# First gate and up weights in two transfers of two contraction blocks each, ahead of the index table, in a fused spectral and gated-MLP kernel

## The chip, the cores and the metric

The kernel runs on one core of a Trainium2 chip. The metric is the device time of one execution in microseconds. Before the change the median of 8 runs is 178.51 us (178.4 to 178.95). A profile is one further execution, recorded by the hardware profiler; its times are counted from the start of its span.

## The reference, cut to what matters

```python
xn = _layernorm(x, axis=-1)                       # x: 2048 x 512
# branch A: a filter in the frequency domain
X = jnp.fft.rfft2(xn.astype(jnp.float32), axes=(-2, -1))
A = jnp.fft.irfft2(X * (w_r + 1j * w_i), s=(2048, 512), axes=(-2, -1))
# branch B: a gated MLP, w_gate and w_up 512 x 1792, w_down 1792 x 512
g = jnp.einsum("bsd,df->bsf", xn, w_gate)
u = jnp.einsum("bsd,df->bsf", xn, w_up)
B = jnp.einsum("bsf,fd->bsd", gelu(g) * u, w_down)
return x + A + B
```

## The kernel before

The 2048 rows are cut into 16 "columns" c of 128 rows each (row 16 p + c lies on partition p). A column of x is 128 x 512 in bf16, 128 KB. Four columns make one block `sb` of 512 rows. The hidden width of 1792 is cut into 14 blocks f of 128, the contraction over 512 into 4 blocks e of 128.

**Branch B.** For each row block and each f, TensorE (PE) forms `g_ps` and `u_ps`, each as four matmuls over e (line 490; line 498 for the very first unit, which runs e 0 and 1 for all its blocks and then e 2 and 3). ScalarE (ACT) turns `g_ps` into `ge` (line 503), VectorE (DVE) multiplies `u_ps` by `ge` into `hT` (line 508). After the whole of this and of branch A, the down projection `y_ps` (line 817) runs over the 14 blocks, the last step of branch A is added into the same PSUM tile (line 821), DVE adds x (line 824), and SyncE (SP) stores.

**Branch A.** The two-dimensional transform and its inverse are chains of small matmuls `bp`, `dp`, `ep`, `gp`, `yp`, with copies on ACT, multiplications by the filter tables `TW` on DVE, and an exchange of partition halves by DMA (line 729). The tables are gathered on GpSimd (POOL) with the row numbers in `idx_t` (line 594).

**Who decides the order.** A planner (`Plan`, lines 135 to 198) takes every step with its engine, its estimated duration, its key and a due time `t_min`, and writes out a static order for each engine. `LAND`, `WG_LAND`, `WU_LAND` and `RF_LAND` (lines 308 to 312) are the landing times that it assumes for the x columns, the weights and a table. They are not waits of the program: those are on semaphores. The list `todo` (line 532) gives the units of branch B: first column 0 with f 0 to 3, then column 1 with f 0 to 3, columns 0 and 1 with f 4 to 5 and with f 6 to 7, then columns 2 and 3 with f 0 to 7 in pairs, columns 0 to 3 with f 8 to 13, and after that the other row blocks.

**The opening.** SP issues all loads, on one hardware queue, in the order of lines 281 to 306: columns 0 and 1 (one each), the index table, gate weights of f 0 to 3 for all four e (512 KB), the up weights of the same (512 KB), columns 2 and 3, gate and up weights of f 4 to 7 (512 KB each), further columns, the weights of f 8 to 13 (768 KB each), and then the remaining columns and tables. The program gives these transfers eight completion semaphores in turn, so a transfer is issued after the one eight places ahead of it has landed.

Meanwhile PE runs 37 filler matmuls on zeros (line 320); DVE takes mean and variance of column 0 and of column 1 (lines 339 and 342) and normalizes (line 345); PE transposes (line 351), DVE copies the result into `xnT` (line 354), and six more filler matmuls follow column 0 (line 324). Columns 2 and 3 go the same way a little later, with the reciprocal root on POOL (lines 357 and 361). The later columns are transposed by DMA (line 455).

Of the kernel before, what the change touches and what calls it, by code (L numbers as in the profile page):

```python
# [10 lines left out]
P = 128  # L11
# [3 lines left out]
ALU = mybir.AluOpType  # L15
AF = mybir.ActivationFunctionType
# [3 lines left out]
NC = 16  # L20
NG = 8
NE = 4
DF = 1792
NFC = DF // P
NSB = 4
EPS = 1e-5
# [108 lines left out]
class Plan:  # L135
# [6 lines left out]
    def add(self, eng, occ, fn, deps=(), key=0.0, lat=None, slack=0.0, t_min=0.0, acq=(), rel=(), after=None):  # L142
        lat = occ + 0.25 if lat is None else lat
        op = Op(len(self.ops), eng, occ, lat, fn, [d for d in deps if d is not None], key, slack, t_min, acq, rel,
                after)
        self.ops.append(op)
        return op
# [54 lines left out]
def kernel(  # L202
# [11 lines left out]
    nc = tc.nc  # L214
    const_np, ccols, rf_np, ri_np, idx_np = _tables()
    cap = nc.inline_tensor(const_np, name="spec_consts").ap()
    rf_d = nc.inline_tensor(rf_np, name="spec_rf").ap()
# [14 lines left out]
    Wg_sb = pc.tile([P, NE, DF], BF16, name="Wg_sb")  # L232
    Wu_sb = pc.tile([P, NE, DF], BF16, name="Wu_sb")
# [6 lines left out]
    W = 257  # L240
# [7 lines left out]
    def load_consts(first, last):  # L248
        a, b = ccols[first][0], sum(ccols[last])
        nc.sync.dma_start(out=CT[:, a:b], in_=cap[:, a:b])  # L250


    def load_x(c0, n, eng=nc.sync):
        eng.dma_start(out=x_t[:, c0:c0 + n, :], in_=x_v[:, c0:c0 + n, :])

    def load_w(a, b, eng=nc.sync):
        nc.sync.dma_start(out=Wg_sb[:, :, a:b], in_=wg_v[:, :, a:b])
        eng.dma_start(out=Wu_sb[:, :, a:b], in_=wu_v[:, :, a:b])
# [1 line left out]
    eps_t = pc.tile([P, 1], F32, name="eps_t")  # L260
    spin = pc.tile([P, P], BF16, name="spin")
    warm = pc.tile([P, 1], F32, name="warm")
    nc.vector.memset(spin[:], 0.0)
    nc.vector.memset(eps_t[:], EPS)
    minus_half = pc.tile([P, 4], F32, name="minus_half")
    nc.vector.memset(minus_half[:], -0.5)
    ident_t = pc.tile([P, P], BF16, name="ident_t")
    nc.gpsimd.memset(ident_t[:], 1.0)
    nc.gpsimd.affine_select(out=ident_t[:], in_=ident_t[:], pattern=[[-1, P]], compare_op=ALU.is_equal, fill=0.0,
                            base=0, channel_multiplier=1)  # L270

    def load_x(c0, n, eng=nc.sync):
        return eng.dma_start(out=x_t[:, c0:c0 + n, :], in_=x_v[:, c0:c0 + n, :])  # L273

# [1 line left out]
        v = wg_v if T is Wg_sb else wu_v  # L276
        return eng.dma_start(out=T[:, e, a:b], in_=v[:, e, a:b])  # L277

    pin = tc.keep_in_program_order
    pin(nc.scalar.activation(out=warm[:], in_=eps_t[:], func=AF.Sqrt, bias=eps_t[:], scale=1.0))  # L280
    pin(load_x(0, 1))
    pin(load_x(1, 1))
    idx_t = pc.tile([P, 3], I32, name="idx_t")
    nc.sync.dma_start(out=idx_t[:], in_=nc.inline_tensor(idx_np, name="spec_rows").ap())  # L284
    load_w(Wg_sb, 0, 512)
    load_w(Wu_sb, 0, 512)
    load_x(2, 2)
    load_w(Wg_sb, 512, 1024)
    load_w(Wu_sb, 512, 1024)
    load_x(4, 2)  # L290
    load_x(6, 2)
    load_w(Wg_sb, 1024, DF)
    load_w(Wu_sb, 1024, DF)
    load_x(8, 2)
    load_x(10, 2)
    for c in range(0, NC, 8):
        nc.sync.dma_start(out=RF_t[:, c:c + 8], in_=rf_d.rearrange("p (c k) -> p c k", c=NC)[:, c:c + 8])
    load_x(12, 2)
    load_x(14, 2)
    load_consts("F0", "L0")  # L300
    load_consts("I0", "M0")
    for T, w_in in ((TR, A_w_r), (TI, A_w_i)):
        rows = w_in.rearrange("(kb a h g) k -> h kb a (g k)", kb=NC, h=2, a=8)
        Tf = T.rearrange("p j k -> p (j k)")
        for h in range(2):
            nc.sync.dma_start(out=Tf[64 * h:64 * h + 64, W:8 * W], in_=rows[h, :, 0:4, W:8 * W])

    LAND = {0: 2.9, 1: 3.6, 2: 8.4, 3: 8.4}
    LAND.update({c: 11.5 if c < 8 else 17.5 if c < 12 else 20.5 for c in range(4, NC)})
    WG_LAND = [6.3] * 4 + [10.2] * 4 + [13.2] * 6  # L310
    WU_LAND = [7.4] * 4 + [11.7] * 4 + [15.2] * 6
    RF_LAND = 19.0

    ident = ident_t[:]
# [1 line left out]
    IQ = [cc(f"I{q}") for q in range(4)]  # L316

    sp_ps = ps.tile([P, D], F32, name="sp_ps", tag="S", bufs=4)
    for k in range(37):
        pin(nc.tensor.matmul(sp_ps[:, :P], lhsT=spin[:], rhs=spin[:], start=True, stop=True))  # L320

    def spin_on():
        for k in range(6):
            nc.tensor.matmul(sp_ps[:, :P], lhsT=spin[:], rhs=x_t[:, 0, :P], start=True, stop=True)
# [3 lines left out]
    add = plan.add  # L328
# [8 lines left out]
    def f_stats(c):  # L337
        tiles["st", c] = st = pw.tile([P, V.BN_STATS_DIM], F32, name="stats", bufs=4)
        V.bn_stats(out=st[:], in_=x_t[:, c, :])  # L339
# [34 lines left out]
    def first_two():  # L374
        o = {}

        def v(k, fn, occ, deps=(), lat=None, t_min=0.0):
            o[k] = add("DVE", occ, fn, [o[d] for d in deps], key=-2000 + len(o), lat=lat, t_min=t_min,
                       after=o.get("last"))
            o["last"] = o[k]  # L380

        def T(c, h):
            o["T", c, h] = add("PE", 0.12, lambda: f_T(c, 2 * h, 2), [o["xn", c, h]], key=-2000 + 2 * c + h,
                               lat=0.36, acq=("S",))

        def xn_(c, h):
            v(("xn", c, h), lambda: f_norm_v(c, 256 * h, 256), 0.27, [("recip", c)], lat=0.4)

        def stats(c):
            v(("stats", c), lambda: f_stats(c), 0.6, t_min=LAND[c], lat=0.7)  # L390

        def mean(c):
            v(("mean", c), lambda: f_mean(c), 0.17, [("stats", c)])
            o["root", c] = add("ACT", 0.31, lambda: A.activation(
                out=rstd[:, c:c + 1], in_=mv[:, c, 1:2], func=AF.Sqrt, bias=eps_t[:], scale=1.0),
                [o["mean", c]], key=-2000 + c)

        def recip(c):
            v(("recip", c), lambda: V.reciprocal(out=rstd[:, c:c + 1], in_=rstd[:, c:c + 1]), 0.15, [("root", c)])

        stats(0)
        mean(0)
        stats(1)

        recip(0)
        xn_(0, 0)
        mean(1)
        xn_(0, 1)
        T(0, 0)
        T(0, 1)  # L410
        add("PE", 0.33, spin_on, [o["T", 0, 1]], key=-1500, lat=0.33, after=o["T", 0, 1])
        table = add("ACT", 1.3, lambda: None, [o["root", 1]], key=-1500, lat=1.3)
        v("copy0", lambda: f_Tc(0, 0, 2), 0.25, [("T", 0, 0)], lat=0.4)
        o["copy0"].rel = ("S",)
        xT_op[0, 0] = o["copy0"]
        recip(1)
        v("copy1", lambda: f_Tc(0, 2, 2), 0.25, [("T", 0, 1)], lat=0.4)
        o["copy1"].rel = ("S",)
        xT_op[0] = o["copy1"]
        xn_op[0] = o["xn", 0, 1]  # L420
        v("xn1", lambda: f_norm_v(1, 0, D), 0.33, [("recip", 1)], lat=0.45)
        t = add("PE", 0.23, lambda: f_T(1, 0, NE), [o["xn1"]], key=-1998, lat=0.45, acq=("S",))
        o["t"] = t
        v("copyt", lambda: f_Tc(1, 0, NE), 0.5, ["t"])
        o["copyt"].rel = ("S",)
        xT_op[1] = o["copyt"]
        xn_op[1] = o["xn1"]

    ROOT = 1.1
    first_two()  # L430

    def moments(c, key):
        s = add("DVE", 0.6, lambda: f_stats(c), key=key, t_min=LAND[c] if c < 4 else max(LAND[c], 14.7))
        return add("DVE", 0.1, lambda: f_mean(c), [s], key=key - 0.5)

    def second_two():
        m = [moments(c, -1200 + c) for c in (2, 3)]
        m = add("POOL", ROOT, lambda: root_eps(2, 2), m, key=-1190, lat=ROOT + 0.1)
        for c in (2, 3):
            xn_op[c] = add("DVE", 0.33, lambda c=c: f_norm_v(c, 0, D), [m], key=-1180 + c, lat=0.53)  # L440
            t = add("PE", 0.23, lambda c=c: f_T(c, 0, NE), [xn_op[c]], key=-880 + c, lat=0.5, acq=("S",))
            e, f = ("ACT", A.copy) if c == 2 else ("DVE", V.tensor_copy)
            xT_op[c] = add(e, 0.5, lambda c=c, f=f: f_Tc(c, 0, NE, f), [t], key=-1100 + c, rel=("S",))
# [26 lines left out]
    def unit(k, c0, n, f0, m=1):  # L470
# [41 lines left out]
        def split(name, tag, W_, key, t, h):  # L512
            o = None
            for f in range(0, m, h):
                o = add("PE", occ * h / m, lambda f=f: mm(name, tag, W_, range(f, f + h)), [o] if f else src, key=key,
                        lat=occ * h / m + 0.3, acq=() if f else (tag,), t_min=t[f0 + f + h - 1])
            return o
# [3 lines left out]
            g = add("PE", occ / 2, lambda: mm_half(1), [xT_op[0], g], key=1000.1, lat=occ / 2 + 0.3)  # L521
        else:
            g = split("g_ps", "G", Wg_sb, 1000 + k, WG_LAND, m)
        u = split("u_ps", "U", Wu_sb, 1003.1 if k == 2 else 1000.5 + k, WU_LAND, (2, m, 1)[k] if k < 3 else m)
        ge = add("ACT", {1: 0.28, 2: 0.36, 4: 0.5}[n * m], f_ge, [g], key=-1000 + k,
                 lat={1: 0.38, 2: 0.48, 4: 0.7}[n * m], acq=("ge",), rel=("G",))
        h = add("DVE", {1: 0.21, 2: 0.34, 4: 0.61}[n * m], f_h, [ge, u], key=-1000 + k, rel=("U", "ge"))
# [318 lines left out]

    E_ = mybir.EngineType
    with tc.manual_schedule(engines={E_.PE, E_.DVE, E_.Activation, E_.Pool, E_.SP}):
        for op in plan.order():
            op.fn()  # L850

# [29 lines left out]
```

## Time and profile before

| | |
|---|---|
| median of 8 runs | 178.51 us |
| the profiled execution | 178.73 us |
| its span | 177.0 us |
| granted TensorE clock | 1.00 |
| instructions | 3114 |
| HBM read, written | 13.38 MB, 2.10 MB |

How to read it: "busy" is the time in which an engine had an instruction running. PEld is PE's weight load, which runs beside its matmuls. A name such as `L490 PE MATMUL u_ps<-xnT,Wu_sb` gives line, engine, operation, and output and inputs by the program's names; `x264` counts instructions. Behind an arrow stands what ended an idle time. In the windows view each row is a stretch of the span, with the busy time of PE, PEld, DVE, ACT and POOL and the instructions of each in brackets, then the granted clock, the mean busy share of the 16 DMA engines, and what they moved in GB/s. "SPq" is the queue in which SP issues transfers; "to landing" is the time from an issue to the completion of its transfer. The chain is the work that ended last, followed back from the last instruction.

### The profile page before, as it was taken

The numbers are of one execution on the slowest core, as the hardware profiler recorded it, in microseconds if no ns is written. First come the engines' busy times: TensorE is split into PE (matmuls) and PEld (weight loads), VectorE is DVE, ScalarE is ACT, GpSimd is POOL, SyncE is SP. The second block draws the span as 40 slices with busy tenths as digits, with TensorE's granted clock in tenths as the row PEclk, the third lists the DMA queues.
The fourth block names the chain that finished last, engine by engine and source line by source line (L and its number), as shares of the span: only waits on it lengthen the run. The fifth ranks groups of instructions, "written<-read, shape, count | busy, mean of one in ns | idle before, by whom it ended". The sixth has DMA issues, their size and how long they took to land.

```text
span 177.0 us, 3114 instructions
## 1 busy us (share of the span) xinstructions
PE 171.5 (97%) x1127; PEld 96.7 (55%) x1145; DVE 116.0 (66%) x255; ACT 95.9 (54%) x170; POOL 17.2 (10%) x38
## 2 busy tenths in 40 slices
PE   7899999999999999999999999999999999999993
PEld 7698845455544554555555455454445445444463
DVE  3588999987434599979899999643516325344333
ACT  4442489799746988898899964362112111211200
POOL 1020340505760000000000000000000000000000
PEclk9999999999999999999999999999999999999999
DMA  3999997433817802211201520200122222221212
GB/s 91 354 378 377 377 180 120 89 62 72 254 34 227 310 0 59 59 30 35 59 17 44 138 61 15 59 0 4 58 90 89 76 76 61 78 99 60 79 43 59
DMA packets 21871, 19.35 MB, mean 109 GB/s; under 512 B 8480, under 2 KB 20000, under 8 KB 21856
## 3 DMA queue, kind: packets, MB, share of 16 engines
q1 hardware_dynamic: 21440, 17.84, 35.3%
q0 software_dynamic: 416, 1.32, 2.6%
q8 instruction: 9, 0.15, 0.3%
q14 instruction: 6, 0.05, 0.1%
HBM read 13.38 MB, written 2.10 MB: 87 GB/s over the span
## 4 chain that ended last, share of the span: by engine, by line
PE 93%; DMA 3%; SPq 1%; issue 1%; DVE 0%
PE u_ps L490 27%; PE y_ps L817 27%; PE g_ps L490 27%; DMA Wu_sb<-in_B_w_up_dram 3%; PE yp L768 2%; PE gp L738 2%; PE dp L635 2%; PE bp L577 2%; PE y_ps L821 2%; PE ep L644 2%; SPq L273 0%; PE tp L351 0%; SPq L277 0%; SPq L284 0%; DVE y_sb L824 0%
## 5 line engine op out<-in xcount | busy, mean ns | idle before, releaser
L490 PE MATMUL u_ps<-xnT,Wu_sb 128*128 128x512 bf16 (+2 forms) x264 | 56.5, 340 | 0.5
L490 PE MATMUL g_ps<-xnT,Wg_sb 128*128 128x512 bf16 (+2 forms) x252 | 55.8, 349 | 0.2
L817 PE MATMUL y_ps<-Wd_sb,hT 128*128 128x512 bf16 (+2 forms) x246 | 50.6, 355 | 0.3
L508 DVE TENSOR_TENSOR hT<-u_ps,ge 128x512 bf16<-128x512 f32 x56 | 38.4, 688 | 18.2 <-PE u_ps L490 15.7
L503 ACT ACTIVATE ge<-g_ps 128x512 bf16<-128x512 f32 x56 | 33.7, 601 | 24.5 <-PE g_ps L490 21.4
L490 PEld LDWEIGHTS <-Wu_sb 128*128 128x128 bf16 x272 | 24.9, 98 | 21.0 <-DMA Wu_sb<-in_B_w_up_dram 0.3
L817 PEld LDWEIGHTS <-hT 128*128 128x128 bf16 x252 | 23.2, 98 | 22.4
L490 PEld LDWEIGHTS <-Wg_sb 128*128 128x128 bf16 x256 | 24.0, 98 | 20.6
L774 ACT CAST yf<-yp 128x512 bf16<-128x512 f32 x16 | 9.3, 586 | 40.5 <-PE yp L768 40.5
L824 DVE TENSOR_TENSOR y_sb<-y_ps,y_sb 128x512 bf16<-128x512 f32 (+2 forms) x18 | 11.1, 631 | 30.1 <-PE y_ps L821 30.1
L649 ACT CAST E<-ep 64x512 bf16<-64x512 f32 x32 | 18.5, 579 | 1.4 <-PE ep L644 1.0
L339 DVE BATCH_NORM_STATS2 stats<-x_t 128x6 f32<-128x512 bf16 x16 | 10.3, 673 | 2.4 <-DMA x_t<-in_A_x_dram 2.4
L452 ACT ACTIVATE xn<-x_t,nb,rstd 128x512 bf16<-128x512 bf16 x12 | 9.5, 811 | 1.0 <-POOL nb L370 1.0
L547 ACT CAST ds<-dp 128x512 bf16<-128x512 f32 x16 | 9.2, 597 | 0.8 <-PE dp L635 0.8
L547 ACT CAST Gs<-gp 128x512 bf16<-128x512 f32 x16 | 8.7, 591 | 0.6 <-PE gp L738 0.5
L547 ACT CAST Bs<-bp 128x512 bf16<-128x512 f32 x16 | 8.3, 607 | 0.5 <-PE bp L577 0.5
L780 DVE TENSOR_TENSOR lv<-yf 128x512 bf16<-128x512 bf16 x16 | 6.1, 421 | 1.5 <-ACT yf L774 0.7
L768 PEld LDWEIGHTS <-Gs 128*128 128x128 bf16 x64 | 4.8, 98 | 3.5
L787 DVE TENSOR_TENSOR yt<-lv 128x512 bf16<-128x512 bf16 x16 | 6.1, 421 | 0.3
L768 PE MATMUL yp<-CT,Gs 128*128 128x128 bf16 x64 | 6.0, 219 | 0.1
L821 PE MATMUL y_ps<-yt,RI_t 128*128 128x512 bf16 (+2 forms) x18 | 6.1, 355 | 0.0
L559 DVE TENSOR_TENSOR A<-xn 128x1024 bf16<-128x1024 bf16 x8 | 5.2, 675 | 1.0 <-ACT xn L452 1.0
(65 smaller groups left out, 119.1 us busy)
## 6 DMA issues: line engine op xcount, KB each, us to landing
F<-F SPq DMA_DIRECT2D x32, 64.0 KB, 2.0
y_sb<-in_A_x_dram SPq DMA_DIRECT2D x16, 128.0 KB, 2.1
out_dram<-y_sb SPq DMA_DIRECT2D x15, 128.0 KB, 1.7
x_t<-in_A_x_dram SPq DMA_DIRECT2D x7, 256.0 KB, 8.9
Wd_sb<-in_B_w_down_dram SPq DMA_DIRECT2D x1, 1792.0 KB, 7.7
Wg_sb<-in_B_w_gate_dram SPq DMA_DIRECT2D x2, 512.0 KB, 5.4
Wu_sb<-in_B_w_up_dram SPq DMA_DIRECT2D x2, 512.0 KB, 6.4
Wg_sb<-in_B_w_gate_dram SPq DMA_DIRECT2D x1, 768.0 KB, 9.9
```

The lines of the kernel that those rows point to most:

```text
L339: V.bn_stats(out=st[:], in_=x_t[:, c, :])
L452: xn_op[c] = add("ACT", 0.72, lambda c=c: A.activation(out=xn[:, c, :], in_=x_t[:, c, :], func=AF.Identity, bias=nb[:, c:c + 1], scale=rst ...
L490: T_.matmul(b[name][:, f], lhsT=W_[:, e, (f0 + f) * P:(f0 + f + 1) * P], rhs=rhs[:, e, :], start=(e == 0), stop=(e == NE - 1))
L503: A.activation(out=b["ge"][:], in_=b["g_ps"][:], func=AF.Gelu_apprx_tanh)
L508: V.tensor_tensor(out=hT_of(sb, f0, m, o, w), in0=b["u_ps"][:], in1=b["ge"][:], op=ALU.mult)
L547: A.copy(out=o, in_=i)
L649: A.copy(out=b["E"][64 * h:64 * h + 64, r], in_=b["ep", h][64 * r:64 * r + 64])
L768: T_.matmul(t[:, q], lhsT=late["G"][:, q, c0 + j], rhs=IQ[q], start=(q == 0), stop=(q == 3), skip_group_check=True)
L774: A.copy(out=b["yf"][:, j], in_=b[j][:])
L817: T_.matmul(b[o][:], lhsT=hT_of(sb, f, 1, cl * P, P)[:, 0], rhs=Wd_sb[:, f, o:o + w], start=(f == 0), stop=False)
L821: T_.matmul(b[o][:], lhsT=late["RI"][:, c, :], rhs=late["yt"][:, c, o:o + w], start=False, stop=True)
L824: V.tensor_tensor(out=b["y"][:, o:o + w], in0=b[o][:], in1=b["y"][:, o:o + w], op=ALU.add)
```

## The change

The weights of f 0 to 3 are loaded in two transfers of two e blocks (256 KB) for the gate and two for the up matrix. The index table is loaded after the x columns, the table `RF` in one transfer where there were two, and the last four x columns in one where there were two. All fills, loads and filler matmuls of the opening are put into a function that runs at the start of the hand-scheduled region. The planner gets other landing times for the first columns and weights; the key of unit 2's up half becomes that of the other units; and the statistics of columns 2 and 3 are ordered behind the last copy of column 1.

```diff
-    pin(load_x(0, 1))
-    pin(load_x(1, 1))
-    nc.sync.dma_start(out=idx_t[:], in_=nc.inline_tensor(idx_np, name="spec_rows").ap())
-    load_w(Wg_sb, 0, 512)
-    load_w(Wu_sb, 0, 512)
-    load_x(2, 2)
...
-    for c in range(0, NC, 8):
-        nc.sync.dma_start(out=RF_t[:, c:c + 8], in_=rf_d.rearrange("p (c k) -> p c k", c=NC)[:, c:c + 8])
-    load_x(12, 2)
-    load_x(14, 2)
...
-    LAND = {0: 2.9, 1: 3.6, 2: 8.4, 3: 8.4}
+    def opening():
+        nc.vector.memset(spin[:], 0.0)
...
+        nc.scalar.activation(out=warm[:], in_=eps_t[:], func=AF.Sqrt, bias=eps_t[:], scale=1.0)
+        load_x(0, 1)
+        load_x(1, 1)
+        for e in range(0, NE, 2):
+            load_w(Wg_sb, 0, 512, e=slice(e, e + 2))
+        for e in range(0, NE, 2):
+            load_w(Wu_sb, 0, 512, e=slice(e, e + 2))
+        load_x(2, 2)
+        load_w(Wg_sb, 512, 1024)
+        load_w(Wu_sb, 512, 1024)
+        load_x(4, 2)
+        load_x(6, 2)
+        load_w(Wg_sb, 1024, DF)
+        load_w(Wu_sb, 1024, DF)
+        load_x(8, 2)
+        load_x(10, 2)
+        nc.sync.dma_start(out=RF_t[:], in_=rf_d.rearrange("p (c k) -> p c k", c=NC))
+        load_x(12, 4)
+        nc.sync.dma_start(out=idx_t[:], in_=nc.inline_tensor(idx_np, name="spec_rows").ap())
...
+        for k in range(37):
+            nc.tensor.matmul(sp_ps[:, :P], lhsT=spin[:], rhs=spin[:], start=True, stop=True)
+
+    LAND = {0: 2.9, 1: 3.6, 2: 7.2, 3: 7.2}
     LAND.update({c: 11.5 if c < 8 else 17.5 if c < 12 else 20.5 for c in range(4, NC)})
-    WG_LAND = [6.3] * 4 + [10.2] * 4 + [13.2] * 6
-    WU_LAND = [7.4] * 4 + [11.7] * 4 + [15.2] * 6
+    WG_LAND = [5.0] * 4 + [8.6] * 4 + [13.2] * 6
+    WU_LAND = [6.2] * 4 + [10.0] * 4 + [15.2] * 6
...
-        m = [moments(c, -1200 + c) for c in (2, 3)]
+        m = [moments(c, -1200 + c, chain_end) for c in (2, 3)]
...
-        u = split("u_ps", "U", Wu_sb, 1003.1 if k == 2 else 1000.5 + k, WU_LAND, (2, m, 1)[k] if k < 3 else m)
+        u = split("u_ps", "U", Wu_sb, 1000.5 + k, WU_LAND, (2, m, 1)[k] if k < 3 else m)
...
     with tc.manual_schedule(engines={E_.PE, E_.DVE, E_.Activation, E_.Pool, E_.SP}):
+        opening()
         for op in plan.order():
             op.fn()
```

More of the change, by code (lines that the diff above doesn't have):

```diff
@@ L262 @@
     warm = pc.tile([P, 1], F32, name="warm")
-    nc.vector.memset(spin[:], 0.0)
-    nc.vector.memset(eps_t[:], EPS)
     minus_half = pc.tile([P, 4], F32, name="minus_half")
-    nc.vector.memset(minus_half[:], -0.5)
     ident_t = pc.tile([P, P], BF16, name="ident_t")
-    nc.gpsimd.memset(ident_t[:], 1.0)
-    nc.gpsimd.affine_select(out=ident_t[:], in_=ident_t[:], pattern=[[-1, P]], compare_op=ALU.is_equal, fill=0.0,
-                            base=0, channel_multiplier=1)
     def load_x(c0, n, eng=nc.sync):
@@ L277, in load_w @@
         return eng.dma_start(out=T[:, e, a:b], in_=v[:, e, a:b])
-    pin = tc.keep_in_program_order
-    pin(nc.scalar.activation(out=warm[:], in_=eps_t[:], func=AF.Sqrt, bias=eps_t[:], scale=1.0))
-    pin(load_x(0, 1))
-    pin(load_x(1, 1))
     idx_t = pc.tile([P, 3], I32, name="idx_t")
-    nc.sync.dma_start(out=idx_t[:], in_=nc.inline_tensor(idx_np, name="spec_rows").ap())
-    load_w(Wg_sb, 0, 512)
-    load_w(Wu_sb, 0, 512)
-    load_x(2, 2)
-    load_w(Wg_sb, 512, 1024)
-    load_w(Wu_sb, 512, 1024)
@@ L290 @@
[L290 to L295, printed above, removed]
-    for c in range(0, NC, 8):
-        nc.sync.dma_start(out=RF_t[:, c:c + 8], in_=rf_d.rearrange("p (c k) -> p c k", c=NC)[:, c:c + 8])
-    load_x(12, 2)
-    load_x(14, 2)
[L300 to L306, printed above, removed]
@@ L308 @@
-    LAND = {0: 2.9, 1: 3.6, 2: 8.4, 3: 8.4}
+    def opening():
+        nc.vector.memset(spin[:], 0.0)
+        nc.vector.memset(eps_t[:], EPS)
+        nc.vector.memset(minus_half[:], -0.5)
+        U = nc.gpsimd
+        U.memset(ident_t[:], 1.0)
+        U.affine_select(out=ident_t[:], in_=ident_t[:], pattern=[[-1, P]], compare_op=ALU.is_equal, fill=0.0,
+                        base=0, channel_multiplier=1)
+        nc.scalar.activation(out=warm[:], in_=eps_t[:], func=AF.Sqrt, bias=eps_t[:], scale=1.0)
[17 more added lines that the diff above has]
+        nc.sync.dma_start(out=idx_t[:], in_=nc.inline_tensor(idx_np, name="spec_rows").ap())
+        load_consts("F0", "L0")
+        load_consts("I0", "M0")
+        for T, w_in in ((TR, A_w_r), (TI, A_w_i)):
+            rows = w_in.rearrange("(kb a h g) k -> h kb a (g k)", kb=NC, h=2, a=8)
+            Tf = T.rearrange("p j k -> p (j k)")
+            for h in range(2):
+                nc.sync.dma_start(out=Tf[64 * h:64 * h + 64, W:8 * W], in_=rows[h, :, 0:4, W:8 * W])
+        for k in range(37):
+            nc.tensor.matmul(sp_ps[:, :P], lhsT=spin[:], rhs=spin[:], start=True, stop=True)
@@ L318 @@
     sp_ps = ps.tile([P, D], F32, name="sp_ps", tag="S", bufs=4)
-    for k in range(37):
-        pin(nc.tensor.matmul(sp_ps[:, :P], lhsT=spin[:], rhs=spin[:], start=True, stop=True))
     def spin_on():
@@ L427, in first_two, with moments @@
         xn_op[1] = o["xn1"]
+        return o["copyt"]
     ROOT = 1.1
-    first_two()
-    def moments(c, key):
-        s = add("DVE", 0.6, lambda: f_stats(c), key=key, t_min=LAND[c] if c < 4 else max(LAND[c], 14.7))
+    chain_end = first_two()
+    def moments(c, key, after=None):
+        s = add("DVE", 0.6, lambda: f_stats(c), key=key, t_min=LAND[c] if c < 4 else max(LAND[c], 14.7), after=after)
         return add("DVE", 0.1, lambda: f_mean(c), [s], key=key - 0.5)
     def second_two():
-        m = [moments(c, -1200 + c) for c in (2, 3)]
+        m = [moments(c, -1200 + c, chain_end) for c in (2, 3)]
         m = add("POOL", ROOT, lambda: root_eps(2, 2), m, key=-1190, lat=ROOT + 0.1)
```

## The prediction

> **What bounds the kernel now.** I read the page first, then the waits of the tensor engine (PE, and PEld for its weight loads), then the opening in one-microsecond windows, then the timeline of the first 13 us, and last the stage between 90 and 112 us, where other engines are nearly full. The page's first part and its chain say that this is a PE kernel:
>
> ```profile
> PE 171.5 (97%) x1127; PEld 96.7 (55%) x1145; DVE 116.0 (66%) x255; ACT 95.9 (54%) x170; POOL 17.2 (10%) x38
> ...
> PE 93%; DMA 3%; SPq 1%; issue 1%; DVE 0%
> ```
>
> PE is 93% of the chain; the only other piece of size is 3% of DMA, and the chain in order of time places it: from 2.65 to 7.92 us, the first up weights. From 7.96 on PE has no named wait until the end at 174. So a change can gain only before 7.96 us, and loses only where it makes PE wait later. The waits of the weight loads price the opening:
>
> ```profile
> PEld L498 <- DMA Wg_sb<-in_B_w_gate_dram: 0.8, 1, 0.8
> PEld L490 <- DMA Wu_sb<-in_B_w_up_dram: 0.3, 1, 0.3
> PEld L351 <- DVE xn L345: 0.2, 1, 0.2
> ```
>
> The two DMA waits are 0.77 and 0.32 us by the timeline, 1.09 together; both lie ahead of 7.96. That is the most that earlier weights can give. In the windows (columns: busy time of PE, PEld, DVE, ACT, POOL, clock, DMA share, GB/s) one sees why the weights are late:
>
> ```profile
> 2.00:3.00 1.00, 1.00 (x12) 1.00 (x11) 0.00 (x1) 0.37 (x2) 0.00 (x0) 1.00 0.83 239
> 3.00:4.00 1.00, 1.00 (x12) 1.00 (x10) 0.97 (x3) 0.06 (x1) 0.00 (x0) 1.00 0.56 67
> 4.00:5.00 1.00, 1.00 (x13) 0.92 (x11) 0.96 (x5) 0.24 (x1) 0.00 (x0) 1.00 0.87 275
> 5.00:6.00 1.00, 0.89 (x12) 0.55 (x10) 0.94 (x6) 0.93 (x2) 0.00 (x0) 1.00 1.09 379
> ```
>
> After the two first columns the transfers fall to 67 GB/s and reach 379 only at 5 us; then the queue is full and everything behind lands in order of issue, at that rate. The trough lies behind the index table, a transfer of 1.5 KB that holds SP's queue for 0.42 us:
>
> ```profile
> 1.71 0.42 SPq L284 DMA_DIRECT2D idx_t<-spec_rows  x1
> ...
> 2.18 0.43 SPq L277 DMA_DIRECT2D Wg_sb<-in_B_w_gate_dram  x1
> ...
> 7.96 0.90 PEld L490 LDWEIGHTS <-Wu_sb 128*128 128x128 bf16 x16 [0.32 <-DMA Wu_sb<-in_B_w_up_dram]
> ...
> 8.73 1.29 DVE L339 BATCH_NORM_STATS2 stats<-x_t 128x6 f32<-128x512 bf16 x2 [0.45 <-DMA x_t<-in_A_x_dram]
> ```
>
> Issue plus time to landing gives the landings: first gate weights 2.18 + 4.3 = 6.5, second 3.75 + 6.5 = 10.25, first up weights 7.95, second 4.23 + 7.5 = 11.73; columns 2 and 3 at 8.73.
>
> **The change, part by part.** *The index table leaves the head of the queue.* The first weight issue moves from 2.18 to about 1.71: 0.47 us. Its use is the gather on POOL at 42 us; even behind the first x columns it has over 20 us of cover. Cost nothing, unless it lands after 42.
>
> *The trough.* Against the 379 GB/s of the next window, the window 3 to 4 lacks 312 KB and the window 4 to 5 lacks 104 KB: 416 KB, or 1.10 us of streaming. The weights now follow the x columns with no small transfer between, and come in pieces of half the size. The trace doesn't show what a 256 KB piece of 1 KB rows does at the start of a busy queue, so I bound the shift S of the whole stream: at least 0.47 (the trough keeps its length and only starts sooner), at most 0.47 + 1.10 = 1.57 (it vanishes). The nearest row is that of the first x column: 128 KB took 2.2 us from issue to landing against 4.3 for 512 KB, so a smaller first piece does ramp sooner. Between the ends I take a little over half the trough, S = 1.1. Below 0.47 I go only if pieces cost something in themselves.
>
> They would by a rule of the Trainium skill that speaks against this change: DMA: Bandwidth & Descriptors, "Rules for kernel authors", asks for 1 MiB or more per DMA, and its anatomy section puts some 2.0 us of fixed cost on each (fitted there for GpSimd's transfers). If the two added pieces paid that one after the other, the up weights would land 4 us later less 1.1. The row speaks otherwise: the seven 256 KB transfers of x, the majority of them queued among the weights, lie inside windows of 375 to 386 GB/s from 10 to 20 us. Behind other transfers the fixed part is covered, and what remains is SP's issue, about 0.43 us a piece, against 0.70 us to stream 256 KB at 375. SP stays ahead. I take nothing for the split, and keep 0.1 for the range.
>
> *PE in the opening.* The first gate unit waits for its copies of the transposed x, not for weights, once S is over 0.4: copy 0 ends at 5.60, copy 1 at 5.92, the filler matmuls' loads end at 5.76. So it starts at 5.76, not 6.53; its second half needs the second gate piece by 6.2, which lands at 6.5 - 1.1 = 5.4. The transposes of column 1 follow, and the first up unit could start 1.09 sooner, at 6.87. Its third matmul needs the second up piece (each output block runs over all four contraction blocks): 7.95 - 1.1 = 6.85. No wait.
>
> *The new order behind it.* The planner is given earlier landing times, and the key of the third up unit is removed. By the built program PE now runs gate blocks 4 to 5, then up blocks 4 to 5, then the transposes of columns 2 and 3; before, gate 4 to 7 and the transposes came ahead of any of these up blocks. From the first up unit to this up unit there are three units of 0.88 (loads at 7.96, 8.81, 9.71, 10.60) and half of a double one, 0.88: 3.52. It is reached at 6.87 + 3.52 = 10.39, and needs the second up weights, which land at 11.73 - 1.1 = 10.63. A new wait of 0.24. Before, these were first used at 12.79, with 1.05 to spare. So the gain is S - 0.24, and at most 1.09: 0.86 here. The other needs fit: second gate weights at 9.51 against a landing at 9.15; transposes of columns 2 and 3 at 11.5 against normalized columns at 11.90 - 1.1 and 12.26 - 1.1.
>
> *Edits at no cost.* The fills and the 37 filler matmuls keep their place at the head of each engine; the extra `after` on columns 2 and 3 leaves VectorE's order there as it was. RF in one transfer is used at 29 us and came by 21; columns 12 to 15 in one are used after 24 us; the constants wait for a slot of the queue in another order and are used at 54. If that cover were gone, each would cost its delay one for one. SP has the same 24 opening transfers (two splits, two merges).
>
> *The middle.* With PE 0.86 sooner and the spectral steps placed half a unit later in its order, those steps fall at almost the same time as before. Here ACT and VectorE are the full engines:
>
> ```profile
> 90.00:96.00 6.00, 6.00 (x42) 3.22 (x40) 5.77 (x15) 5.92 (x12) 0.00 (x0) 1.00 0.19 45
> ...
> 102.00:108.00 6.00, 5.95 (x33) 2.85 (x32) 5.84 (x14) 3.22 (x6) 0.00 (x0) 1.00 0.19 45
> ```
>
> and for the exchange through SP (the tile's own view from 90 to 118 us: issues, then time to landing):
>
> ```profile
> L729 SPq DMA_DIRECT2D F<-F x16: 461/595/602, 91.1 to 113.3; - x16
> ...
> DMA to landing us min/median/max: 1.9/2.0/2.1
> ```
>
> The last exchange is issued at 113.3 and lands at 115.3; PE's last `gp` loads come at 116.25. That is 0.9 us of slack, and PE wants it 0.86 sooner: just enough. VectorE waited 2 us for PE's `u_ps` between 78 and 98, which an earlier PE gives back, and one more of its products stands ahead of the first spectral step. I take no loss; the bounds are 0 and about 0.5.
>
> **Sum.** The profiled execution took 178.73 with a span of 177.0, so 1.73 lie around it. 178.73 - 0.86 = 177.87 for it; the median of the runs is 0.22 below it, so 178.51 - 0.86 = 177.65.
>
> **Rivals.** *The trough only moves* (S of 0.47 to 0.8): the gain is 0.23 to 0.56, with a longer wait at the second up weights; 178.1. For it: nothing shows that the ramp depends on the index table. Against: the x column's faster landing. *The gain is given back* in the middle, or pieces cost as much as they save: 178.4, no change that can be told. For it: ACT at 99% from 90 to 96. *Slower: the spectral chain takes over.* The reordered products delay VectorE's last exchange; PE waits at the last `gp`, and the inverse transform behind it waits too. Place: 115 us. The price is one for one past the 0.9 us of slack; from 1.3 us of delay of that landing the kernel is slower by over 0.2%. Two products of 0.69 us pushed ahead of the chain would do it: 179.0. Against: VectorE has 2 us of waits to recover.
>
> **How the numbers follow.** 0.2% is 0.36 us, about what a measurement of this kernel can tell from no change. Likeliest case, gain 0.6 to 1.1: 0.58. Trough only moves: 0.20, two thirds of it beyond 0.36. Given back: 0.12. Slower: 0.10. So faster 0.72, same 0.18, slower 0.10. The range is from 177.35 (all of 1.09 and a little noise) to 178.45, which leaves out the slower case and the edge of the third.
>
> **What would show it.** Right: first up unit's loads at 6.9, a PEld wait of some 0.2 on up weights near 10.4, no wait of over 0.2 at the last `gp`, span 176.1. Wrong: loads at 7.4 or later (trough kept), gate wait still there (split costs), or a gap of PE between 84 and 118.

## The result, and the profile after

The changed kernel takes 180.06 us (median of 21 runs, 178.93 to 181.01) against 178.62 for the kernel before in the same comparison (57 runs, 178.39 to 179.79): a ratio of 1.007, 95% interval 1.0058 to 1.0081. It is slower by about 1.3 us where the prediction had it faster by 0.86. Its profiled execution took 179.92 with a span of 178.2, against 178.73 and 177.0: 1.2 us more in both, so the profile holds the loss.

The page's first part and the chain's shares of the changed kernel:

```profile
PE 171.9 (96%) x1127; PEld 96.6 (54%) x1145; DVE 115.9 (65%) x255; ACT 95.6 (54%) x170; POOL 17.2 (10%) x38
...
PE 91%; DMA 3%; DVE 2%; SPq 1%; issue 1%; DVEq 0%
```

PE's work is the same to 0.4 us; the chain holds a little less PE. The waits of the weight loads say where it stood still (line, what it waited for: us in total, times, longest):

```profile
PEld L491 <- DMA Wu_sb<-in_B_w_up_dram: 1.9, 3, 0.7
...
PEld L491 <- DMA Wg_sb<-in_B_w_gate_dram: 0.3, 1, 0.3
```

Before, the two DMA waits were 1.09 together. The wait for the first gate weights is gone, but there are now four waits for other weights, 0.64, 0.57, 0.34 and 0.73 by the timeline, 2.3 in all. The timeline of the changed kernel places them (start, duration, engine, line, operation, and in brackets the idle time before it and what ended that):

```profile
5.81 0.94 PEld L499 LDWEIGHTS <-Wg_sb 128*128 128x128 bf16 x16
...
7.61 0.11 PEld L491 LDWEIGHTS <-Wu_sb 128*128 128x128 bf16 x2 [0.64 <-DMA Wu_sb<-in_B_w_up_dram]
...
8.29 0.78 PEld L491 LDWEIGHTS <-Wu_sb 128*128 128x128 bf16 x14 [0.57 <-DMA Wu_sb<-in_B_w_up_dram]
...
9.04 0.94 PEld L491 LDWEIGHTS <-Wg_sb 128*128 128x128 bf16 x16
...
9.59 1.29 DVE L339 BATCH_NORM_STATS2 stats<-x_t 128x6 f32<-128x512 bf16 x2 [1.98 <-DMA x_t<-in_A_x_dram]
...
9.93 0.94 PEld L491 LDWEIGHTS <-Wu_sb 128*128 128x128 bf16 x16
...
11.21 0.77 PEld L491 LDWEIGHTS <-Wg_sb 128*128 128x128 bf16 x8 [0.34 <-DMA Wg_sb<-in_B_w_gate_dram]
...
12.70 0.77 PEld L491 LDWEIGHTS <-Wu_sb 128*128 128x128 bf16 x8 [0.73 <-DMA Wu_sb<-in_B_w_up_dram]
...
15.68 0.32 PEld L491 LDWEIGHTS <-Wg_sb 128*128 128x128 bf16 x3
```

and in the kernel before the unit behind the first up unit, and the first gate unit of columns 2 and 3 (the changed kernel's stands at 15.68):

```profile
8.81 0.94 PEld L490 LDWEIGHTS <-Wg_sb 128*128 128x128 bf16 x16
...
14.49 0.86 PEld L490 LDWEIGHTS <-Wg_sb 128*128 128x128 bf16 x8
```

Add up against before, whose first up unit began at 7.96 and whose PE then ran without a wait, 0.88 a unit. The first up unit began at 7.61 but stood still for its second piece; the next unit starts at 9.04 where before it was 8.81: 0.23 lost. The unit after next would start at 10.82 and starts at 11.21: 0.39. The next would start at 12.09 and starts at 12.70: 0.61. That is 1.23, the whole difference of the spans. From 12.7 on both kernels run at PE's pace. By the first gate unit of columns 2 and 3 the changed kernel is 1.19 behind, and from there to the first weight load of `y_ps` (119.03 before, 120.22 after) both take 104.54. The window from 90 to 96 us is as full as before.

```profile
90.00:96.00 6.00, 6.00 (x40) 3.18 (x40) 5.80 (x14) 5.90 (x12) 0.00 (x0) 1.00 0.19 45
```

The page's chain puts its 3% of DMA on columns 2 and 3 and not on weights, because VectorE finished normalizing column 2 at 12.69, just as PE went on. The up unit at 12.70 is of columns 0 and 1 and doesn't read that result, and the second up weights landed at 12.66; so the wait is theirs.

So the transfers were late. Windows of the changed kernel (PE, PEld, DVE, ACT, POOL, clock, DMA share, GB/s), to be held against those of before in the prediction:

```profile
2.00:3.00 1.00, 1.00 (x12) 1.00 (x11) 0.00 (x0) 0.37 (x2) 0.00 (x0) 1.00 0.93 250
3.00:4.00 1.00, 1.00 (x12) 1.00 (x10) 0.87 (x3) 0.00 (x0) 0.00 (x0) 1.00 0.80 197
4.00:5.00 1.00, 1.00 (x12) 0.91 (x9) 0.96 (x5) 0.29 (x1) 0.00 (x0) 1.00 1.03 325
5.00:6.00 1.00, 0.96 (x15) 0.71 (x14) 0.94 (x7) 0.82 (x2) 0.00 (x0) 1.00 0.98 328
6.00:7.00 1.00, 1.00 (x21) 0.97 (x18) 0.35 (x2) 0.79 (x2) 0.00 (x0) 1.00 0.92 287
7.00:8.00 1.00, 0.43 (x5) 0.11 (x2) 0.42 (x1) 0.56 (x1) 0.00 (x0) 1.00 0.83 222
8.00:9.00 1.00, 0.70 (x13) 0.71 (x14) 0.00 (x0) 0.00 (x0) 0.00 (x0) 1.00 1.05 323
```

and the three rows of before that go with the last three:

```profile
6.00:7.00 1.00, 0.47 (x9) 0.47 (x10) 0.24 (x1) 0.65 (x1) 0.00 (x0) 1.00 1.11 389
7.00:8.00 1.00, 0.85 (x16) 0.68 (x14) 0.14 (x1) 0.37 (x1) 0.00 (x0) 1.00 0.99 298
8.00:9.00 1.00, 1.00 (x19) 1.00 (x20) 0.55 (x2) 0.23 (x1) 0.00 (x0) 1.00 1.04 355
```

The trough from 3 to 5 us did fill in part, by 130 + 50 = 180 KB. But from 5 to 9 us the stream is short by 51 + 102 + 76 + 32 = 261 KB. It isn't SP: the second up piece was issued at 3.21 and columns 2 and 3 at 3.72, so the queue had work all the time. Read from the trace, each transfer ends in 16 completions, as many as the core has DMA engines, and I take each for one engine's. A wait ends with the last of them: in the changed kernel the statistics of columns 2 and 3 begin at 9.59, and the last completion is at 9.56. The table has the last of them, and in brackets the time from the first to the last (us; "/" between pieces):

| | before | after |
|---|---|---|
| column 0 | 2.98 (0.38) | 3.08 (0.44) |
| column 1 | 3.39 (0.29) | 3.78 (0.63) |
| first gate weights | 6.48 (0.91) | 5.09 (0.99) / 5.77 (0.87) |
| first up weights | 7.92 (0.78) | 7.57 (1.75) / 8.25 (1.73) |
| columns 2, 3 | 8.71 (0.82) | 9.56 (2.18) |
| second gate weights | 10.22 (0.92) | 11.16 (2.16) |
| second up weights | 11.71 (0.92) | 12.66 (2.10) |

The first gate weights came 0.71 sooner. From then on the 16 parts of a transfer drift apart, from 0.9 to over 2 us, and what ends last is 0.85 to 0.95 late, though between 2 and 10 us (the last of these windows: 375 before, 343 after) only some 100 KB fewer were moved, 0.27 us at 379 GB/s. Most of the loss is unevenness among the engines, not bytes.

### The profile page after: what moved, and what is told of

It reads as the page before. It is cut to its first block, busy times and chain, and to the rows that moved or that the text cites. A ratio compares the mean times of both kernels' runs of the same rounds, so it can differ in the third digit from the quotient of the medians.

```text
span 178.2 us, 3112 instructions
## 1 busy us (share of the span) xinstructions
PE 171.9 (96%) x1127; PEld 96.6 (54%) x1145; DVE 115.9 (65%) x255; ACT 95.6 (54%) x170; POOL 17.2 (10%) x38
## 4 chain that ended last, share of the span: by engine, by line
PE 91%; DMA 3%; DVE 2%; SPq 1%; issue 1%; DVEq 0%
PE y_ps L818 27%; PE u_ps L491 26%; PE g_ps L491 26%; DMA x_t<-in_A_x_dram 3%; PE dp L636 2%; PE yp L769 2%; PE gp L739 2%; PE bp L578 2%; PE y_ps L822 2%; PE ep L645 2%; SPq L270 1%; DVE stats L339 1%; SPq L266 0%; DVE hT L509 0%; PE tp L351 0%
## 5 line engine op out<-in xcount | busy, mean ns | idle before, releaser
L645 PE MATMUL ep<-ds,CT 128*128 128x512 bf16 x16 | 5.9, 379 | 0.0
```

The lines of the kernel that those rows point to most:

```text
L645: T_.matmul(t[:], lhsT=cc("L" if g + h else "L0"), rhs=b["ds", h][:], start=True, stop=True)
```

## The experiments

The theories, as the expectations name them. **P**: the pieces cost. **P1**: a transfer of 256 KB costs wherever it stands; **P2**: it costs only at the head, while the stream is starting. **Q**: not the pieces, but the table's leaving, crowds the head. Beside these stands the planner's new order as a cost of its own. A ratio is that to the kernel before on the same chip, with its 95% interval; it is worked out from the single runs and is not the quotient of the two medians shown. The experiments ran on two chips, so a difference between two ratios of different chips is less sure than one ratio. One profile of a kernel is one execution, and landings differ by up to 0.7 us between profiles of kernels with the same first transfers (the gate weights of experiments 3 and 6, 6.34 and 5.62), so conclusions rest on the ratios.

**1. Whole first weights, all else as changed.**

```diff
-        for e in range(0, NE, 2):
-            load_w(Wg_sb, 0, 512, e=slice(e, e + 2))
-        for e in range(0, NE, 2):
-            load_w(Wu_sb, 0, 512, e=slice(e, e + 2))
+        load_w(Wg_sb, 0, 512)
+        load_w(Wu_sb, 0, 512)
```

> The changed kernel with the first gate and up weights in one transfer each again; the index table stays late and PE keeps the new order. Theory P (the pieces themselves slow the stream: with each of them the DMA engines lose time, the slowest most): without pieces the stream is 0.4 to 1.0 us ahead of before, second up weights land at 10.8 to 11.3, the median is 177.9 to 178.5. Theory Q (place: weights directly behind the x columns, with no index table between, make one DMA engine lag; the pieces are harmless): as slow as the changed kernel, 179.5 to 180.5, first up weights after 8.1 us.

178.86 against 178.86: 0.9992 (0.9969 to 1.0015), between what P and Q expected. Without the pieces the loss is gone; Q falls. No gain comes either, and its timeline shows why:

```profile
7.53 0.90 PEld L489 LDWEIGHTS <-Wu_sb 128*128 128x128 bf16 x16 [0.30 <-DMA Wu_sb<-in_B_w_up_dram]
...
11.62 0.77 PEld L489 LDWEIGHTS <-Wu_sb 128*128 128x128 bf16 x8 [0.64 <-DMA Wu_sb<-in_B_w_up_dram]
```

The first up unit is 0.43 sooner than before (7.96), and the new order gives that back at the second up weights.

**2. The split alone** (kernel before, with its old order and the table at the front).

```diff
-    load_w(Wg_sb, 0, 512)
-    load_w(Wu_sb, 0, 512)
+    for e in range(0, NE, 2):
+        load_w(Wg_sb, 0, 512, e=slice(e, e + 2))
+    for e in range(0, NE, 2):
+        load_w(Wu_sb, 0, 512, e=slice(e, e + 2))
```

> The kernel before with nothing but the split of the first gate and up weights into two transfers each; index table in front, old landing times, old order of PE. Theory P: the first up weights land 0.3 to 0.6 us later than before (8.3 to 8.6), and the kernel takes 179.0 to 179.6. Theory Q: as before, 178.4 to 178.9, up weights complete at 7.9 to 8.1.

180.36 against 178.86: 1.0078 (1.006 to 1.0097). The split alone costs as much as the whole change, and more than either theory expected. Its profile shows the loss behind the pieces. They landed at 7.06 and 7.87, no later than the whole up weights before (7.92); columns 2 and 3 landed at 9.51, with 1.73 between first and last completion, and PE stood at the second gate weights:

```profile
11.15 1.64 PEld L492 LDWEIGHTS <-Wg_sb 128*128 128x128 bf16 x16 [0.67 <-DMA Wg_sb<-in_B_w_gate_dram]
```

**3. The table alone** (kernel before).

```diff
     load_x(1, 1)
-    nc.sync.dma_start(out=idx_t[:], ...)
     load_w(Wg_sb, 0, 512)
...
     load_x(14, 2)
+    nc.sync.dma_start(out=idx_t[:], ...)
```

> The kernel before with only the index table moved behind the x columns; weights whole, old landing times, old order of PE. Theory P: the stream comes 0.4 to 1.0 us sooner, the first up weights at 7.0 to 7.5, and the kernel takes 177.7 to 178.2. Theory Q: the engines lag, first up weights at 8.0 or later, 178.7 to 179.5.

178.43 against 178.86: 0.9971 (0.9959 to 0.9984), the only kernel whose interval lies below the kernel before; P had expected a larger gain. The windows and first loads of its profile:

```profile
3.00:4.00 1.00, 1.00 (x12) 1.00 (x10) 0.91 (x3) 0.00 (x0) 0.00 (x0) 1.00 0.69 117
4.00:5.00 1.00, 1.00 (x12) 0.91 (x9) 0.96 (x5) 0.29 (x1) 0.00 (x0) 1.00 1.03 345
5.00:6.00 1.00, 0.99 (x12) 0.58 (x10) 0.83 (x6) 0.87 (x2) 0.00 (x0) 1.00 1.06 373
```

```profile
6.38 0.90 PEld L498 LDWEIGHTS <-Wg_sb 128*128 128x128 bf16 x16 [0.57 <-DMA Wg_sb<-in_B_w_gate_dram]
...
7.81 0.90 PEld L490 LDWEIGHTS <-Wu_sb 128*128 128x128 bf16 x16 [0.30 <-DMA Wu_sb<-in_B_w_up_dram]
```

The trough is 120 KB smaller from 3 to 5 us, nothing is lost behind it, and the up unit is 0.15 sooner (7.96 before).

**4. The changed kernel with the planner of before.**

```diff
-    LAND = {0: 2.9, 1: 3.6, 2: 7.2, 3: 7.2}
+    LAND = {0: 2.9, 1: 3.6, 2: 8.4, 3: 8.4}
...
-    WG_LAND = [5.0] * 4 + [8.6] * 4 + [13.2] * 6
-    WU_LAND = [6.2] * 4 + [10.0] * 4 + [15.2] * 6
+    WG_LAND = [6.3] * 4 + [10.2] * 4 + [13.2] * 6
+    WU_LAND = [7.4] * 4 + [11.7] * 4 + [15.2] * 6
...
-        u = split("u_ps", "U", Wu_sb, 1000.5 + k, ...)
+        u = split("u_ps", "U", Wu_sb, 1003.1 if k == 2 else 1000.5 + k, ...)
```

> The changed kernel (split, index table late) with the landing times and the key of before in the planner, so that PE has its order of before: second up weights not used before some 13 us. Under both P and Q the late stream costs at the first up unit and at the second gate weights only, and the new wait at the second up weights goes: about 0.6 us of the loss of 1.4 stays, 179.0 to 179.5. If the order is harmless (rival R: all of the loss is in the landings of the first weights), it stays at 179.8 to 180.3.

179.63 against 178.86: 1.0028 (1.0009 to 1.0047). It stands between experiment 3 and the changed kernel: the pieces at the head cost, and the new order on top of them. (Beside the pieces it has the opening function and the merged transfers of the changed kernel; experiment 6 has these too and is level with before.) Its profiled execution (180.33) is its slowest of 22, which go down to 178.82, and is not used for sizes: there the second up piece landed at 9.65, 1.4 later than in the changed kernel, from the same issues.

**5. Only the gate weights in two pieces** (experiment 3 and this).

```diff
-    load_w(Wg_sb, 0, 512)
+    for e in range(0, NE, 2):
+        load_w(Wg_sb, 0, 512, e=slice(e, e + 2))
```

> The kernel before with the index table late and only the first gate weights in two pieces, up weights whole, old order of PE. If each added transfer at the head costs alike (both P1 and P2 below), half of the split's cost shows: 0.2 to 0.35% over the kernel with the index table late and nothing split, so about as the kernel before, 178.5 to 179.0. If only the second split hurts, 178.3 to 178.5; if the first does all the harm, 179.2 or more.

180.12 (5 runs) against 178.44: 1.0087 (1.0074 to 1.01). One split costs more than two did in experiment 4, so the costs don't add. Windows of its profile, and the first up unit:

```profile
5.00:6.00 1.00, 0.94 (x14) 0.78 (x15) 0.94 (x6) 0.90 (x2) 0.00 (x0) 1.00 0.82 267
6.00:7.00 1.00, 1.00 (x20) 0.90 (x17) 0.28 (x1) 0.79 (x2) 0.00 (x0) 1.00 0.85 244
7.00:8.00 1.00, 0.08 (x2) 0.00 (x0) 0.42 (x1) 0.49 (x1) 0.00 (x0) 1.00 0.89 226
```

```profile
8.94 0.89 PEld L491 LDWEIGHTS <-Wu_sb 128*128 128x128 bf16 x16 [2.04 <-DMA Wu_sb<-in_B_w_up_dram]
```

Gate pieces landed at 4.72 and 5.63, the second no later than the whole weights in the best case (5.62 in experiment 6); the 512 KB behind them took until 8.90, with 2.42 between its first and last completion. It is 1.16% above experiment 3, measured on the other chip.

**6. The same cut three transfers later** (experiment 1, with the second gate and up weights in two pieces each).

```diff
-        load_w(Wg_sb, 512, 1024)
-        load_w(Wu_sb, 512, 1024)
+        for T in (Wg_sb, Wu_sb):
+            for e in range(0, NE, 2):
+                load_w(T, 512, 1024, e=slice(e, e + 2))
```

> The changed kernel with the first gate and up weights whole, and instead the second ones (blocks 4 to 7) in two pieces each; same number of transfers and bytes, PE in the new order, so that it waits for exactly these weights near 11.6 us. Theory P1 (an added 256 KB piece costs the DMA engines time wherever it stands): as slow as the changed kernel, 179.6 to 180.4. Theory P2 (pieces cost only at the start, while few transfers are queued behind each other): as the unsplit kernel of this order, 178.6 to 179.1.

178.42 against 178.44: 0.9999 (0.9991 to 1.0007), as experiment 1. The same number of added pieces of the same size, with the queue full ahead of them, costs nothing that can be told, though PE waits for just these weights: P1 falls. Its windows and PE:

```profile
4.00:5.00 1.00, 1.00 (x13) 1.00 (x11) 0.96 (x5) 0.18 (x2) 0.00 (x0) 1.00 1.04 367
5.00:6.00 1.00, 1.00 (x13) 0.89 (x12) 0.75 (x5) 0.98 (x2) 0.00 (x0) 1.00 1.07 377
6.00:7.00 1.00, 1.00 (x22) 1.00 (x20) 0.30 (x1) 0.58 (x1) 0.00 (x0) 1.00 1.11 372
```

```profile
7.17 0.90 PEld L490 LDWEIGHTS <-Wu_sb 128*128 128x128 bf16 x16
...
11.42 0.55 PEld L490 LDWEIGHTS <-Wu_sb 128*128 128x128 bf16 x6 [0.58 <-DMA Wu_sb<-in_B_w_up_dram]
```

In this execution the head went as the prediction wanted, with no piece in it: up unit at 7.17, 0.79 sooner than before. Then the new order waited 0.58 for the second up weights.

**7. A second small transfer at the head** (kernel before, the index table in two).

```diff
-    nc.sync.dma_start(out=idx_t[:], in_=nc.inline_tensor(idx_np, name="spec_rows").ap())
+    idx_d = nc.inline_tensor(idx_np, name="spec_rows").ap()
+    nc.sync.dma_start(out=idx_t[:, 0:2], in_=idx_d[:, 0:2])
+    nc.sync.dma_start(out=idx_t[:, 2:3], in_=idx_d[:, 2:3])
```

> The kernel before with the index table in two transfers (two columns and one column, 1 KB and 0.5 KB) at the same early place; nothing split, old order. If the count of transfers at the head is what costs, whatever their size, this added one costs what the first one does, 0.3 to 0.5 us: 178.9 to 179.4. If the pieces of weights cost by something of their own, a tiny transfer of more costs nothing: within 0.15 of the kernel before.

179.23 (5 runs) against 178.44: 1.0045 (1.0032 to 1.0058), 0.8 us. The windows show a trough that grew, not a slow stream:

```profile
3.00:4.00 1.00, 1.00 (x12) 1.00 (x10) 0.97 (x3) 0.07 (x1) 0.00 (x0) 1.00 0.38 22
4.00:5.00 1.00, 1.00 (x13) 0.94 (x11) 0.96 (x5) 0.22 (x1) 0.00 (x0) 1.00 0.68 140
5.00:6.00 1.00, 0.91 (x12) 0.56 (x10) 0.91 (x6) 0.94 (x2) 0.00 (x0) 1.00 1.08 372
```

The time between first and last completion stays at 0.6 for the first weights. The time is what the count of transfers would make it, but experiments 6 and 10 speak against the count as a rule. A tiny transfer at the head and a piece of 256 KB thus cost in two ways: one delays the start, the other lets the 16 parts of a transfer drift apart.

**8. Up pieces issued by ScalarE** (changed kernel), so that neither SP's issue nor its one queue is between the pieces.

```diff
         load_x(1, 1)
+        for e in range(0, NE, 2):
+            load_w(Wu_sb, 0, 512, nc.scalar, e=slice(e, e + 2))
         for e in range(0, NE, 2):
             load_w(Wg_sb, 0, 512, e=slice(e, e + 2))
-        for e in range(0, NE, 2):
-            load_w(Wu_sb, 0, 512, e=slice(e, e + 2))
```

> The changed kernel with the two first up pieces issued by ScalarE (behind its first table load, at 2.4 and 2.9 us) instead of SP; all else as changed. If SP's issues or its one queue are what starves the stream, the up pieces land sooner and columns 2 and 3 as well: 178.6 to 179.4. If the DMA engines lose the time on the pieces themselves, it stays at 179.6 to 180.4.

179.69 (6 runs) against 178.44: 1.0073 (1.0054 to 1.0092), as the changed kernel. It is not a clean exchange: ScalarE issued at 1.05 and 1.54, not at 2.4 and 2.9, so the up pieces (4.37 and 6.12) landed ahead of the gate pieces (6.31 and 7.25), and column 1 beside them only at 4.67. DVE took it up at 4.69 (3.93 in the changed kernel):

```profile
4.69 0.69 DVE L339 BATCH_NORM_STATS2 stats<-x_t 128x6 f32<-128x512 bf16 x1 [0.82 <-DMA x_t<-in_A_x_dram]
...
7.29 0.45 PEld L499 LDWEIGHTS <-Wg_sb 128*128 128x128 bf16 x8 [0.19 <-DMA Wg_sb<-in_B_w_gate_dram]
```

All four pieces had landed 1.0 sooner than in the changed kernel (7.25 against 8.25), yet columns 2 and 3 came at 9.45, again with 2.40 between first and last completion. So SP's issue is not what drives the engines apart.

**9. Only the up weights in two pieces** (experiment 3 and this).

```diff
-    load_w(Wu_sb, 0, 512)
+    for e in range(0, NE, 2):
+        load_w(Wu_sb, 0, 512, e=slice(e, e + 2))
```

> The kernel before with the index table late, gate weights whole and only the first up weights in two pieces; old order of PE. The mirror of the gate-only split, which cost 0.9% against before. If a piece costs by standing first behind the x columns, this is harmless: 178.2 to 178.5, as the unsplit one. If any piece near the head costs alike, about as bad as the gate-only split: 179.3 to 180.2.

179.14 against 178.83: 1.002 (1.0001 to 1.0039), 0.49% above experiment 3. One place further back the split costs less than that of the gate weights. The profiled execution (178.74) is its fastest, and shows that the pieces need not drift: up pieces at 6.38 and 7.09, 0.4 between first and last completion. The up unit then came as early as the prediction wanted, and PE waited at the second gate weights (landed 10.18):

```profile
7.07 0.94 PEld L491 LDWEIGHTS <-Wu_sb 128*128 128x128 bf16 x16
...
10.22 1.64 PEld L491 LDWEIGHTS <-Wg_sb 128*128 128x128 bf16 x16 [0.43 <-DMA Wg_sb<-in_B_w_gate_dram]
```

**10. Fewer transfers at the head** (experiment 3, with columns 0 and 1 in one).

```diff
-    pin(load_x(0, 1))
-    pin(load_x(1, 1))
+    pin(load_x(0, 2))
```

> The kernel before with the index table late and columns 0 and 1 in one transfer of 256 KB; weights whole, old order. If what counts is the number of transfers ahead of the weights, the stream comes another 0.3 to 0.5 us sooner and the up weights land at 7.3 to 7.5; column 0 lands with column 1 at 3.4, which delays the first gate unit to some 6.3 but not the up unit: 177.9 to 178.3, faster than with the index table late alone. If the count is not it, the later column 0 is all that is left: 178.4 to 178.9.

179.14 against 178.83: 1.0038 (1.0017 to 1.006). The runs fall into two groups, 13 from 178.78 to 179.28 and 9 from 180.29 to 180.60. The profiled one (180.59) is of the upper group: column 0 was only there at 4.23, and the time from first to last completion reached 2.42, with no weights cut at all. So the number of transfers at the head isn't the rule either.

**11. Four pieces each** (experiment 3, first gate and up weights by single e).

```diff
-    load_w(Wg_sb, 0, 512)
-    load_w(Wu_sb, 0, 512)
+    for T in (Wg_sb, Wu_sb):
+        for e in range(NE):
+            load_w(T, 0, 512, e=slice(e, e + 1))
```

> The kernel before with the index table late and the first gate and up weights in four pieces each (one contraction block, 128 KB a piece); old order. If every added transfer at the head costs its issue on SP and more, six added ones make 2 to 4 us: 180.5 to 182.5. If two pieces already do all the harm (an engine that falls behind once, whatever follows), 179.2 to 180.2.

180.67 (6 runs) against 178.83: 1.0103 (1.0068 to 1.0138), the highest ratio of all, though its interval overlaps those of experiments 2 and 5. The first quarter lands at 4.22, the last up quarter only at 8.85, columns 2 and 3 at 10.82 with 3.13 between first and last completion.

## Why the prediction was wrong, point by point

**"I take nothing for the split, and keep 0.1 for the range": this step failed.** With the old order the split takes experiment 3 from 0.9971 to experiment 4's 1.0028: 0.57% or 1.0 us (experiment 2, with the table in front: 0.78%, 1.4 us). I had costed it by the x transfers at 375 to 386 GB/s between 10 and 20 us. That row is right for a full queue, and experiment 6 confirms it there; I carried it to the head, where the queue was not yet full. The Trainium skill (DMA: Bandwidth & Descriptors, "Rules for kernel authors") asks for 1 MiB or more per DMA. Its direction was right at the head and had no measurable effect deeper in the queue. The same page ("Anatomy of one DMA") has about 2.0 us of fixed cost per transfer, fitted for those that GpSimd issues; two of them one after the other would be 4 us, by that estimate, and neither place shows it.

**The shift S = 1.1: failed with it.** S was one number for the whole stream. By the table it was 0.71 at the gate weights, -0.33 at the up weights, -0.85 to -0.95 at what came after. The step of 0.47 for the table was held to be a sure floor; moving the table alone gained 0.29% or 0.5 us in the runs, which fits, and only 0.15 us in its one profile. The "x column's faster landing" was a sound guess for the first piece alone (5.09). The end of the last piece, and of all behind it, decides.

**The first gate unit at 5.76: right** (5.81). **The first up unit at 6.87, "No wait": wrong**, 7.61 and then 8.29, because the second up piece landed at 8.25 and not at 6.85. The sign set for a costly split, a gate wait that stays, did not come: the split's cost showed only behind the gate weights. Loads at 7.4 or later did come, but not from a trough that was kept.

**A new wait of 0.24 at the second up weights: right in place, too small.** 0.73 by the load, 0.61 of PE's time. I had seen that the order gave up 1.05 us of cover and priced it with weights that land at 10.63; they landed at 12.66. (The rival with a smaller S expected a longer wait here; by the prediction's own sum S moves both ends alike, and the wait stays 0.24.) In the runs the new order costs 0.42% or 0.75 us on top of the pieces (1.0028 to 1.007, intervals apart, but from two comparisons); with whole weights it is 0.21% (experiments 3 and 1, intervals overlapping). Its wait of 0.6 appears in experiments 1 and 6 too.

The terms by the runs: table -0.5, pieces +1.0, order +0.75, together +1.25 us or 0.7%, in place of -0.86. They are differences along one path, so they must add up to the measured ratio. On other paths the pieces cost 1.4 us (the kernel before to experiment 2, or experiment 1 to the changed kernel, 0.78% each) and the rest correspondingly less. So the pieces cost 1.0 to 1.4 us, and the order's share is the less certain.

**The edits at no cost and the middle: right.** Experiments 1 and 6 hold the opening function, the merged transfers and the late table, and are level with before; from 15.68 on the changed kernel keeps the pace of before to 0.01 us, so there is no new wait at the last `gp`, and the spectral chain did not take over. So the slower rival that I had priced, at 115 us, was not the one that came. (The chances sum to 0.71 and 0.19 rather than 0.72 and 0.18; nothing hangs on it.) The nearest was "pieces cost as much as they save", at 0.12, and it was short by the size.

**What stays open.** Why short transfers at the head drive the 16 engines apart. Shown is that it is not SP (8), not the count (6, 10), and not the table (1, 3); that it is worse nearer to the head (5 above 9); and that it doesn't add up (5 above 4). That a finer cut is worse is only suggested (11). Nor are pieces the whole rule: experiment 9's profile has them without the drift, experiment 10's has the drift without them.

The packets of the profiles say a little more. Between 4.5 and 11 us the median packet of 1 KB takes 0.046 us, and one of 2 KB some 0.09. The longest took 1.22 us in the changed kernel and 1.16, 1.21 and 1.05 in experiments 4, 5 and 11, all with drift; in the kernel before and experiments 3, 6 and 7 it took 0.34 to 0.44. In between are experiments 2, 8 and 10, with drift (0.76, 0.64 and 0.55), and 1 and 9, with little (0.59 and 0.62). So single held packets go with the drift in four profiles, but they are not shown to be all of it, nor is what held them. It was no load of instructions: from 0 to 11.5 us the instruction queues moved nothing over 64 bytes in any profile. The trace doesn't name the engine of a packet.

Scatter between runs doesn't settle it: the changed kernel runs from 178.93 to 181.01 and experiment 3, without pieces, from 178.06 to 178.70, but the kernel before reached 180.91 beside it, and experiment 11's six runs lie within 0.5. Only cuts along the contraction blocks e were tried.

## What to carry to other kernels

A split at the head of the queue is to be checked at the landing of its last piece and of the transfers behind it, since a wait ends only with the last of 16 completions; a first piece that comes sooner proves nothing. A bandwidth measured in a full queue (here 375 to 386 GB/s) doesn't carry over to the queue's start (67 and 275 from 3 to 5 us). And a static order should not be retimed to landings that are only hoped for: it turns a late transfer from covered into a stall.

## What the runs showed of the hardware that was not expected

In the kernel before too, the time from first to last completion jumps, from 0.92 to 1.92 us, at the time of one packet of 16 KB on an instruction queue that took 1.13 us (12.13 to 13.26); there it does no harm, since all landings have slack by then. One transfer more at the head, for a table of 1.5 KB in all, cost 0.45% (experiment 7), and one fewer gained 0.29% (experiment 3): 0.5 to 0.8 us for a transfer whose bytes are next to nothing. Merging the first two x columns gave one kernel two separate times, 178.8 to 179.3 and 180.3 to 180.6.
